# A whole order planned anew, with four single banks open to every product

## The chip, the cores and the metric

The kernel runs on one core of a Trainium2 chip. The metric is the device time of one execution in microseconds (us). Lower is better. Five engines work at once, each through a queue of its own in the order written: TensorE (PE, matrix products), VectorE (DVE), ScalarE (ACT), GpSimd (POOL) and SyncE (SP, which here issues all transfers).

## The reference

An attention of the RWKV-6 kind feeds a two-layer network. For 4 sequences of 768 tokens, with 8 heads of 48:

```python
for t in range(S):
    cur = np.einsum('bhd,bhe->bhde', u[None] * kt, vt)
    y[:, :, t] = np.einsum('bhd,bhde->bhe', rt, state + cur)
    state = wt[:, :, :, None] * state + np.einsum('bhd,bhe->bhde', kt, vt)
# x: y as 3072 tokens x 384
h = x @ w_in          # 384 x 2048
r = np.maximum(h, 0.0)
return (r * r) @ w_out    # 2048 x 384
```

Inputs and output are float32.

## The kernel before

**Steps.** The tokens are cut into 12 steps of 256 (three for each sequence), a step into two chunks (c = 0, 1) of 128. Within a chunk the recurrence becomes matrix products. For each step the kernel loads w, k, r and v (384 KB each), and then: ww_ multiplies neighbouring decays, lw_ takes the logarithm, cum_ sums the logarithms on TensorE, al_ derives the second sum, exp_ takes the exponential, rd_ scales k and r (rd_.s.1 and rd_.s.0) with it. kw_, rw_, ku_, qp_, q_, qs_, vs_, v_ and vq_ are elementwise preparations and casts. The scaled k and r are transposed: on TensorE (tr_, copied out by rkt_) for steps 0 to 3, by transfers (dtr_, two for rT and one for kT) for steps 4 to 11. p_ makes the scores of half the heads, pm_ masks them, su_, ts_ and sn_ carry the state, y_ and yc_ make the output, ysb_ brings it to SBUF, and it is transposed by yt_ and xt_ (steps 0 to 5) or by a transfer, dyt_ (steps 6 to 11).

**Network.** m1_.s.g makes 256 of the 2048 hidden columns of step s: six products of 128x256. rl_ takes the ReLU out of PSUM, sq_.s.q squares a quarter of the hidden columns, m2_.s.c.q multiplies that quarter of chunk c with its part of w_out: four products of 128x384, and four m2_ add up in one bank. os_ copies the sum to SBUF, store writes it. The two weights come in four pieces each (ld.g.i for w_in, ld.g.o for w_out; 768 KB), each cast to bf16 by a cast. Piece g of w_in serves m1_.s.2g and m1_.s.2g+1, piece q of w_out serves m2_.s.c.q.

**Order.** All of it stands in one string, ORDER: a word is an operation, its step and parts, after "=" the engine (A is ACT, V is DVE, G is POOL), after ":" the bank. The kernel issues the words in that order, so each engine's queue is the string's order of its own words. SP's queue holds the loads (ld), stores, dtr_ and dyt_. A word waits in its queue until its inputs are there and its buffer is free; what stands behind it on that engine waits too.

**Banks.** PSUM has two double banks (att, written 0 and 1 by the attention's words) and four single ones: bk (2) and m1_bank (2). m1_ takes only m1_bank, m2_ only bk; p_ and su_ can take "m" or "b", a pair of single banks, in place of a double one. Lines 531 to 571 are m1_, rl_, sq_, m2_ and os_; rl_ is line 545 on ACT and 547 on DVE, sq_ 553 and 555, os_ 568 and 570.

**Dummies.** warm_.n.i issues n products on zeros into a bank; they serve no output. They stand only in the opening, 46 products in 8 words.

**Buffers.** Four for each of the loads w, k, r and v, four for weight pieces on their way to the cast, four for outputs.

Of the kernel before, what the change touches and what calls it, by code (L numbers as in the profile page):

```python
# [17 lines left out]
ld.0.w ld.0.k ld.0.r ld.0.u ld.1.w ww_.0=V lw_.0 warm_.11.5 cum_.0:0 kw_.0=G exp_.0 rd_.0.1 ld.0.v warm_.8.5  # L18
tr_.0.1:0 rkt_.0.1=A ld.1.k ld.1.r rw_.0=G ld.2.w ku_.0=G rd_.0.0 ld.1.v warm_.3.5 tr_.0.0:1 ww_.1=V
rkt_.0.0=A qp_.0=V ld.2.r v_.0=A warm_.5.5 p_.0.0:m p_.0.1:1 ac_.0 lw_.1 q_.0 su_.0:b ld.2.k cum_.1:0  # L20
ts_.0.0=A kw_.1=G pm_.0.0 pm_.0.1 vs_.0.0=A sn_.0.0 ld.1.i exp_.1 rw_.1=G vs_.0.1=A qs_.0=A rd_.1.1 ku_.1=G
warm_.3.2 yc_.0.1:1 ld.0.i ac_.1 ts_.0.1=V rd_.1.0 warm_.2.2 tr_.1.1:0 sn_.0.1 y_.0:1 rkt_.1.1=A vq_.0=V
tr_.1.0:1 ww_.2=G ld.2.i v_.1=A rkt_.1.0=V ysb_.0=V vs_.1.1=A warm_.4.2 p_.1.1:0 qp_.1=G su_.1:m ld.2.v
pm_.1.1 lw_.2 yt_.0:0 cum_.2:1 ld.3.i ts_.1.0=V rw_.2=G q_.1 exp_.2 kw_.2=G xt_.0=V vs_.1.0=A rd_.2.0 qs_.1=G
ac_.2 cast.i.1=A rd_.2.1 warm_.10.1 tr_.2.0:1 sn_.1.0 p_.1.0:0 ku_.2=G ts_.1.1=V yc_.1.1:1 tr_.2.1:0
cast.i.0=A pm_.1.0 ld.0.o m1_.0.3:0 ld.3.w rkt_.2.1=V m1_.0.2:1 vq_.1=G rkt_.2.0=V y_.1:1 rl_.0.3=A yc_.1.0:1
rl_.0.2=V p_.2.0:0 m1_.0.1:0 ld.1.o ysb_.1=V cast.i.2=G m1_.0.0:1 rl_.0.1=A pm_.2.0 yt_.1:0 ld.3.r rl_.0.0=A
m1_.0.5:0 v_.2=A xt_.1=V qp_.2=G sn_.1.1 m1_.0.4:1 rl_.0.5=A p_.2.1:1 su_.2:b sq_.0.0=A rl_.0.4=V ld.2.o
m1_.1.4:0 cast.i.3=G ts_.2.0=V pm_.2.1 m1_.1.5:1 rl_.1.4=A q_.2 sn_.2.0 m1_.1.3:0 rl_.1.5=A ld.3.o vs_.2.1=G
vs_.2.0=A yc_.2.0:0 yc_.2.1:0 rl_.1.3=V m1_.1.6:1 cast.o.0=G qs_.2=A m1_.1.0:0 ld.3.k rl_.1.6=V sq_.0.2=A  # L30
y_.2:0 rl_.1.0=V m1_.1.1:1 vq_.2=G m1_.1.7:0 rl_.1.1=V ld.3.v m2_.0.1.0:0 sq_.1.2=A rl_.1.7=V sq_.0.1=A
cast.o.1=G m1_.1.2:1 rl_.1.2=A ysb_.2=V m1_.0.7:0 ld.4.w ww_.3=G yt_.2:1 rl_.0.7=V m1_.0.6:1 xt_.2=V m2_.0.1.1
sq_.1.1=A rl_.0.6=V ld.5.w m1_.2.6:0 cast.o.2=G lw_.3 sq_.1.0=A rl_.2.6=A cum_.3:1 sq_.1.3=A rw_.3=G al_.3
ld.5.r m2_.0.0.0:1 m1_.2.7:1 m2_.0.0.1 cast.o.3=V exp_.3 sq_.0.3=A ld.4.k rd_.3.0 kw_.3=G m1_.2.1:0 rl_.2.7=A
ac_.3 m2_.0.1.2 m2_.0.0.2 rl_.2.1=V ku_.3=G m2_.0.0.3 rd_.3.1 ld.4.v m2_.0.1.3 vs_.3.0=A m1_.2.0:1 os_.0.1=V
qp_.3=G ld.5.v m1_.2.3:0 os_.0.0=V rl_.2.0=V tr_.3.1:0 rl_.2.3=A tr_.3.0:1 rkt_.3.1=V v_.3=A ld.4.r m1_.2.4:1
ww_.4=G rkt_.3.0=V m2_.1.0.0:0 rl_.2.4=A q_.3 ww_.5=G p_.3.1:0 vs_.3.1=A ld.6.k su_.3:1 pm_.3.1 p_.3.0:m
m2_.1.0.1 ts_.3.0=A lw_.4 sn_.3.0 ld.5.k pm_.3.0 m2_.1.0.2 qs_.3=A m2_.1.1.0:1 sq_.2.0=A vq_.3=G ts_.3.1=V
m2_.1.0.3 ld.6.w cum_.4:0 m2_.1.1.1 ku_.4=G ac_.4 al_.4 store.0.1 m1_.2.5:0 os_.1.0=A v_.5=A yc_.3.1:1 y_.3:1
lw_.5 kw_.4=G m1_.2.2:1 ld.6.r ysb_.3=V rl_.2.5=A m2_.1.1.2 exp_.4 sn_.3.1 rl_.2.2=V yt_.3:0 rw_.4=G cum_.5:1  # L40
xt_.3=V m2_.1.1.3 vs_.4.0=A ac_.5 sq_.2.1=A qp_.4=G al_.5 m1_.3.0:0 rd_.4.1 v_.4=A m1_.3.3:1 rd_.4.0 dtr_.4.1
m2_.2.0.0:0 rl_.3.0=A rw_.5=G rl_.3.3=A m2_.2.0.1 os_.1.1=V exp_.5 q_.4 dtr_.4.0 su_.4:0 sq_.2.2=A m1_.3.4:0
kw_.5=G rd_.5.0 ww_.6=G m2_.2.1.0:1 rl_.3.4=A ts_.4.0=V sq_.2.3=A m1_.3.5:1 vs_.4.1=A rd_.5.1 sn_.4.0
m2_.2.1.1 store.1.0 ts_.4.1=V rl_.3.5=V ku_.5=G m1_.3.6:0 store.1.1 m2_.2.1.2 qs_.4=A ld.7.w ld.6.v rw_.6=G
p_.4.1:1 rl_.3.6=A p_.4.0:0 pm_.4.1 pm_.4.0 m2_.2.1.3 lw_.6 vq_.4=G m1_.3.1:1 m1_.3.2:0 rl_.3.1=A su_.5:1
dtr_.5.1 dtr_.5.0 vs_.5.1=G sq_.3.0=A rl_.3.2=V yc_.4.0:0 yc_.4.1:0 sn_.4.1 y_.4:0 os_.2.1=V sq_.3.1=A
m1_.3.7:1 ysb_.4=V ld.7.v m2_.2.0.2 rl_.3.7=A ld.8.w kw_.6=G vs_.5.0=G yt_.4:1 ld.7.k sq_.3.3=A m2_.2.0.3
xt_.4=V cum_.6:0 al_.6 m1_.4.4:0 qp_.5=G os_.2.0=A ac_.6 m1_.4.7:1 ts_.5.0=V exp_.6 rl_.4.4=V m2_.3.0.0:1
rl_.4.7=A rd_.6.1 m1_.4.6:0 rd_.6.0 m2_.3.0.1 dtr_.6.1 m2_.3.1.0:0 ku_.6=G qp_.6=G sq_.3.2=A rl_.4.6=A q_.5
dtr_.6.0 p_.5.0:1 p_.5.1:0 vs_.6.0=A m1_.4.5:1 sn_.5.0 m2_.3.0.2 qs_.5=G rl_.4.5=A pm_.5.1 pm_.5.0 vq_.5=G  # L50
m1_.4.1:0 m1_.4.3:1 rl_.4.3=A store.2.1 ld.8.v m2_.3.0.3 rl_.4.1=V ld.8.k v_.6=A ww_.7=G y_.5:0 q_.6 os_.3.0=A
ld.7.r m1_.4.0:1 store.0.0 ld.9.k ww_.8=G yc_.5.0:0 qs_.6=A su_.6:1 yc_.5.1:0 ysb_.5=V vs_.6.1=A ts_.6.0=V
m1_.4.2:0 ld.8.r m2_.3.1.1 rl_.4.0=V yt_.5:1 xt_.5=V sn_.6.0 lw_.7 vq_.6=G rl_.4.2=A p_.6.0:0 m2_.3.1.2
sq_.4.3=A store.2.0 pm_.6.0 m1_.5.2:1 ku_.7=G m1_.5.6:0 ts_.6.1=V yc_.6.1:0 sq_.4.0=A rl_.5.2=A p_.6.1:1
rl_.5.6=A m2_.3.1.3 kw_.7=G pm_.6.1 sq_.4.2=A m1_.5.4:1 rw_.7=G m1_.5.3:0 os_.3.1=V rl_.5.4=A y_.6:0 sn_.6.1
rl_.5.3=A cum_.7:1 kw_.8=G ysb_.6=V al_.7 m2_.4.0.0:1 vs_.7.1=A m1_.5.7:1 m1_.5.5:0 v_.7=G dyt_.6 sq_.4.1=A
rl_.5.7=V qp_.7=G rl_.5.5=V m2_.4.1.0:0 exp_.7 ld.9.w ld.9.v m2_.4.0.1 ac_.7 rd_.7.0 sq_.5.1=A m2_.4.0.2
ku_.8=G rd_.7.1 sq_.5.3=A dtr_.7.0 m2_.4.0.3 m1_.5.0:1 lw_.8 m1_.5.1:0 rw_.8=G rl_.5.0=V su_.7:0 q_.7
rl_.5.1=A cum_.8:1 dtr_.7.1 m1_.6.3:1 qs_.7=A m1_.6.5:0 rl_.6.3=V ld.10.w qp_.8=G ac_.8 sq_.5.0=A m2_.4.1.1
os_.4.0=V ts_.7.0=V ld.11.w sn_.7.0 m1_.6.4:1 rl_.6.5=A al_.8 ww_.9=G m2_.4.1.2 ld.9.r rl_.6.4=V exp_.8  # L60
store.3.0 m2_.5.1.0:1 sq_.5.2=A rd_.8.1 ts_.7.1=V sn_.7.1 m1_.6.0:0 vs_.7.0=G vs_.9.1=A rd_.8.0 m2_.4.1.3
m2_.5.1.1 kw_.9=G rl_.6.0=A dtr_.8.0 p_.7.1:0 v_.8=A p_.7.0:1 vq_.7=G pm_.7.1 m1_.6.1:1 m2_.5.1.2 rl_.6.1=A
pm_.7.0 ku_.9=G m2_.5.1.3 sq_.6.0=A lw_.9 m1_.6.6:0 dtr_.8.1 store.3.1 q_.8 yc_.7.0:0 v_.9=A yc_.7.1:0
rl_.6.6=V rw_.9=G su_.8:1 y_.7:0 os_.5.1=A ts_.8.0=V m1_.6.2:1 ysb_.7=V os_.4.1=A cum_.9:1 m1_.6.7:0 al_.9
dyt_.7 m2_.5.0.0:1 rl_.6.2=V exp_.9 ww_.10=G rl_.6.7=V m2_.5.0.1 ac_.9 ld.10.r rd_.9.1 sq_.6.1=A sq_.6.2=A
sn_.8.0 qp_.9=G ld.10.k qs_.8=G store.4.1 m2_.5.0.2 ld.10.v rd_.9.0 m2_.5.0.3 m2_.6.1.0:0 vs_.8.1=G sq_.6.3=A
dtr_.9.0 vs_.8.0=A p_.8.0:m p_.8.1:0 pm_.8.0 su_.9:1 m2_.6.1.1 ts_.9.0=A pm_.8.1 m2_.6.1.2 lw_.10 m1_.7.4:0
rw_.10=G os_.5.0=V m1_.7.0:1 rl_.7.4=V sn_.9.0 vq_.8=G yc_.8.1:0 dtr_.9.1 yc_.8.0:0 rl_.7.0=V y_.8:0 m1_.7.1:0
q_.9 rl_.7.1=A ts_.9.1=V m2_.6.1.3 kw_.10=G ysb_.8=V m1_.7.7:1 sq_.7.0=A ww_.11=G cum_.10:1 dyt_.8 rl_.7.7=V
m1_.7.5:0 qs_.9=A al_.10 m2_.6.0.0:1 v_.10=G rl_.7.5=A m1_.7.2:1 exp_.10 ld.11.k vs_.9.0=G m2_.6.0.1 lw_.11  # L70
rd_.10.0 rd_.10.1 m1_.7.3:0 rl_.7.2=A vq_.9=G ac_.10 m2_.6.0.2 os_.6.1=A rl_.7.3=A vs_.10.0=A store.6.1
m1_.7.6:1 store.5.1 ku_.10=G m2_.6.0.3 vs_.10.1=A ld.11.r sn_.9.1 rl_.7.6=V m1_.8.5:0 dtr_.10.0 p_.9.1:0
rl_.8.5=A p_.9.0:1 qp_.10=G pm_.9.1 m1_.8.3:1 m2_.7.0.0:0 rl_.8.3=A pm_.9.0 m1_.8.4:0 sq_.7.1=A m1_.8.2:1
os_.6.0=A y_.9:0 sq_.7.3=A rl_.8.2=V yc_.9.1:0 rw_.11=G su_.10:1 m2_.7.1.0:1 sq_.7.2=A ts_.10.0=V ysb_.9=V
m2_.7.1.1 rl_.8.4=A ku_.11=G q_.10 m1_.8.7:1 dyt_.9 m1_.8.1:0 rl_.8.7=V cum_.11:0 dtr_.10.1 kw_.11=G sn_.10.0
rl_.8.1=A m2_.7.1.2 al_.11 m1_.8.0:1 exp_.11 ld.11.v qs_.10=G ts_.10.1=V sn_.10.1 vq_.10=G m1_.8.6:0 rl_.8.0=A
store.6.0 rd_.11.0 m2_.7.1.3 rl_.8.6=A rd_.11.1 m1_.9.4:1 sq_.8.0=A ac_.11 dtr_.11.0 m1_.9.1:0 qp_.11=G
rl_.9.4=V sq_.8.2=A m2_.7.0.1 os_.7.1=V p_.10.1:1 sq_.8.1=A p_.10.0:0 pm_.10.1 store.5.0 dtr_.11.1 store.7.1
m1_.9.0:1 v_.11=G pm_.10.0 vs_.11.1=G m2_.8.1.0:1 rl_.9.0=A rl_.9.1=A m2_.8.1.1 sq_.8.3=V m1_.9.5:1 m2_.7.0.2
m2_.7.0.3 os_.7.0=A yc_.10.0:1 yc_.10.1:1 rl_.9.5=V su_.11:0 y_.10:1 m1_.9.2:0 ysb_.10=V m1_.9.6:1 rl_.9.2=A  # L80
ts_.11.0=V dyt_.10 m2_.8.0.0:0 rl_.9.6=V sn_.11.0 m1_.9.3:0 q_.11 m2_.8.1.2 rl_.9.3=A yc_.11.0:1 vs_.11.0=A
p_.11.1:0 yc_.11.1:1 p_.11.0:m m2_.8.0.1 pm_.11.0 m2_.8.0.2 pm_.11.1 sq_.9.1=A m2_.8.0.3 m2_.8.1.3 qs_.11=A
# [549 lines left out]
```

## Time and profile before

| | us |
|---|---|
| median of three runs | 183.11 |
| lowest and highest run | 182.49, 183.14 |
| span of the profiled execution | 182.2 |
| PE busy | 171.8 |
| ACT busy | 132.7 |
| DVE busy | 130.0 |
| POOL busy | 122.7 |

The page of the profile gives the span (first to last instruction) and no time of its own for that execution; the median stands 0.91 us above the span. The granted TensorE clock has a mean of 0.997. The 16 DMA engines are busy at a share of 85.9% for the transfers that the kernel issues. In rows of the timeline the first number is the start, the second the length; "[1.84 <-DMA ...]" is idle time before the row and what ended it. In rows of the windows stand the stretch, its length, the busy time of PE, PEld (weight loads), DVE, ACT and POOL with counts, the granted clock, the DMA share and GB/s. In rows of groups stand line, engine, operation, tiles, shapes and count, then busy time and mean ns, then idle time before the group.

### The profile page before, as it was taken

How to read it: one execution, taken by the hardware profiler on the slowest of the kernel's cores; microseconds unless marked ns; L12 is line 12 of the kernel's file. 1: busy time of each engine (PE TensorE's matmuls, PEld its weight loads, DVE VectorE, ACT ScalarE, POOL GpSimd, SP SyncE). 2: the span in 40 equal slices, each digit the busy share in tenths (PEclk: the TensorE clock that was granted, in tenths of full speed). 3: DMA queues.
4: the chain of work that ended last, by engine and by line, in shares of the span. 5: the costliest groups of instructions: out<-in, count | busy, mean ns of one | idle time of the engine just before them, and what ended most of it. 6: DMA issues, size and time to landing. Idle time of an engine off the chain costs nothing.

```text
span 182.2 us, 5695 instructions
## 1 busy us (share of the span) xinstructions
PE 171.8 (94%) x2385; PEld 123.4 (68%) x2385; DVE 130.0 (71%) x195; ACT 132.7 (73%) x235; POOL 122.7 (67%) x140
## 2 busy tenths in 40 slices
...
GB/s 138 263 263 240 221 359 350 337 314 311 234 274 230 261 158 270 99 247 130 239 296 205 193 270 172 252 189 193 171 109 195 150 47 0 86 144 33 0 86 130
DMA packets 79208, 35.81 MB, mean 197 GB/s; under 512 B 72400, under 2 KB 77648, under 8 KB 79184
## 3 DMA queue, kind: packets, MB, share of 16 engines
q1 hardware_dynamic: 79184, 35.46, 85.9%
q8 instruction: 18, 0.29, 0.7%
...
## 4 chain that ended last, share of the span: by engine, by line
PE 75%; SPq 10%; DMA 8%; ACT 4%; issue 1%; DVE 1%; ACTq 0%
PE bk L561 32%; PE m L536 32%; SPq L178 8%; DMA w_st<-in_moe_w_in_dram 5%; PE att L420 3%; DMA rT<-rdec_buf 2%; PE att L483 2%; PE att L493 2%; PE att L446 1%; ACT gt L545 1%; PE att L326 1%; ACT wi_sb L200 1%; PE bk L516 1%; SPq L188 1%; SPq L205 1%
## 5 line engine op out<-in xcount | busy, mean ns | idle before, releaser
L536 PE MATMUL m<-xT,wi_sb 128*128 128x256 bf16 x576 | 74.0, 273 | 1.3 <-ACT gt L545 1.2
L561 PE MATMUL bk<-wo_sb,gt 128*128 128x384 bf16 x384 | 71.9, 326 | 0.0
L536 PEld LDWEIGHTS <-wi_sb 128*128 128x128 bf16 x576 | 54.8, 98 | 13.0 <-issue 0.9
L561 PEld LDWEIGHTS <-gt 128*128 128x128 bf16 x384 | 36.9, 98 | 19.2
L545 ACT ACTIVATE gt<-m 128x512 f16<-128x512 f32 x56 | 33.0, 595 | 22.3 <-PE m L536 21.9
L553 ACT ACTIVATE gt<-gt 128x1024 bf16<-128x1024 f16 x42 | 43.3, 1051 | 1.4 <-DVE gt L547 1.1
L547 DVE TENSOR_SCALAR gt<-m 128x512 f16<-128x512 f32 x40 | 27.0, 686 | 9.6 <-PE m L536 9.3
L434 DVE TENSOR_TENSOR pmT<-att,mask 128x1024 bf16<-128x1024 f32 x20 | 23.9, 1218 | 4.5 <-PE att L420 4.5
L297 POOL TENSOR_TENSOR ku<-k_raw,u_bc 128x768 f32<-128x768 f32 x12 | 21.8, 1819 | 0.2 <-DMA u_bc<-in_u_dram 0.2
L302 POOL TENSOR_TENSOR ku<-ku,r_raw 128x768 f32<-128x768 f32 x11 | 20.7, 1881 | 0.2
L316 POOL TENSOR_TENSOR ku<-v_sh,qs 128x768 f32<-128x768 bf16 x11 | 16.3, 1479 | 4.9 <-ACT qs L277 4.8
L277 ACT CAST v_sh<-v_raw 64x384 bf16<-64x384 f32 x34 | 17.3, 508 | 0.4
L290 POOL TENSOR_TENSOR k_raw<-k_raw,w_raw 128x384 f32<-128x384 f32 x12 | 12.2, 1013 | 6.4 <-DMA k_raw<-in_k_dram 6.3
L286 POOL TENSOR_TENSOR r_raw<-r_raw,w_raw 128x384 f32<-128x384 f32 x12 | 12.0, 1000 | 6.4 <-DMA r_raw<-in_r_dram 6.4
L504 DVE TENSOR_TENSOR y_sb<-att,ku 128x768 bf16<-128x768 f32 x12 | 11.4, 953 | 5.5 <-issue 1.6
L461 POOL TENSOR_TENSOR S<-t_state,ac_buf 128x192 bf16<-128x192 f32 x20 | 10.2, 512 | 6.4 <-DVE t_state L456 3.4
L361 DVE TENSOR_TENSOR kdec_buf<-k_raw,att 128x768 bf16<-128x768 f32 x12 | 11.4, 949 | 3.4 <-ACT att L340 2.8
L358 DVE TENSOR_TENSOR rdec_buf<-r_raw,att 128x384 bf16<-128x384 f32 x24 | 12.1, 547 | 2.2 <-ACT att L340 1.1
L340 ACT ACTIVATE att<-att 128x768 f32<-128x768 f32 x12 | 9.6, 798 | 3.1 <-PE att L328 1.9
L568 ACT ACTIVATE o_sb<-bk 128x384 f32<-128x384 f32 x13 | 6.3, 485 | 7.4 <-PE bk L561 7.3
L307 DVE TENSOR_REDUCE q<-ku 128x16 f32<-128x768 f32 x12 | 11.3, 943 | 0.0
L578 PE MATMUL att<-warm 128*128 128x512 bf16 x27 | 9.1, 492 | 1.2 <-DVE half_ones L228 1.2
...
## 6 DMA issues: line engine op xcount, KB each, us to landing
w_raw<-in_w_dram SPq DMA_DIRECT2D x12, 384.0 KB, 5.3
k_raw<-in_k_dram SPq DMA_DIRECT2D x12, 384.0 KB, 5.9
r_raw<-in_r_dram SPq DMA_DIRECT2D x12, 384.0 KB, 5.7
v_raw<-in_v_dram SPq DMA_DIRECT2D x12, 384.0 KB, 5.8
...
w_st<-in_moe_w_in_dram SPq DMA_DIRECT2D x4, 768.0 KB, 11.1
...
rT<-rdec_buf SPq DMA_TRANSPOSE x16, 4.1
```

The source lines that it names most:

```text
L178: nc.sync.dma_start(out=t[:, hs, at:at + 2, :].rearrange("p h j d -> p h (j d)"), in_=src[b, hs, i * T:(i + 1) * T, :].rearrange("h (p j) ...
L277: copy(out[j * Q:(j + 1) * Q, c], src[c * Q:(c + 1) * Q, :, j])
L290: tensor_mul("kw_", s, h)(raw["k", s][:, hs, 0, :], raw["k", s][:, hs, 1, :], raw["w", s][:, hs, 1, :])
L297: tensor_mul("ku_", s, h)(tiles["ku", s][:, hs], raw["k", s][:, hs, 1:3, :], u_bc[:, hs, None, :].to_broadcast([C, n, 2, D]))
L302: tensor_mul("qp_", s, h)(ku, ku, raw["r", s][:, heads(h), 0:2, :])
L316: tensor_mul("vq_", s)(vq[:], tiles["vs", s][:], tiles["qs", s][:, :, :, None].to_broadcast([C, 2, H, D]))
L434: nc.vector.tensor_mul(pmT, ps_p[:].rearrange("p e (x t) -> p (e x) t", t=C), mk.to_broadcast([C, 8, C]))
L536: nc.tensor.matmul(ps1[:, j, :], wi_sb[:, n // 4, kk, n % 4 * 128:(n % 4 + 1) * 128], tiles["xT", s][:, :, kk, :], start=(kk == 0), stop=( ...
L545: nc.scalar.activation(rl, m1, AF.Relu, scale=RS)
L547: nc.vector.tensor_scalar(out=rl, in0=m1, scalar1=RS, scalar2=0.0, op0=ALU.mult, op1=ALU.max)
L553: nc.scalar.activation(gt, rl, AF.Square)
L561: nc.tensor.matmul(m2, gt[:, n, c * C:(c + 1) * C], wo_sb[:, n, :], start=(n == 0), stop=(n == NT - 1))
```

## The change

It replaces the string ORDER, opens all four single banks to m1_ and m2_ alike (the list `quad`), and lets the four quarters of an m2_ sum come in any order: the first quarter issued starts the sum and the fourth ends it, counted in `summed`.

```diff
+    quad = bk + m1_bank
...
     def m1_(s, g):
-        ps1 = tiles["m1", s, g] = m1_bank[int(slot["m1_", s, g])][:].rearrange("p (j t) -> p j t", j=2)
+        ps1 = tiles["m1", s, g] = quad[int(slot["m1_", s, g])][:].rearrange("p (j t) -> p j t", j=2)
...
+    summed = {}
+
     def m2_(s, c, q):
         gt = tiles["gt", s]
-        m2 = bk[int(slot["m2_", s, c])][:, 0:DM]
-        for n in range(4 * q, 4 * q + 4):
-            nc.tensor.matmul(m2, gt[:, n, c * C:(c + 1) * C], wo_sb[:, n, :],
-                             start=(n == 0), stop=(n == NT - 1))
+        m2 = quad[int(slot["m2_", s, c])][:, 0:DM]
+        summed[s, c] = summed.get((s, c), 0) + 1
+        for n in range(4):
+            nc.tensor.matmul(m2, gt[:, 4 * q + n, c * C:(c + 1) * C], wo_sb[:, 4 * q + n, :],
+                             start=(summed[s, c] == 1 and n == 0), stop=(summed[s, c] == NT // 4 and n == 3))
```

The products, copies and transfers are the same in number; what differs is their order, and on which engine some run:

| words | before: ACT, DVE, POOL | after |
|---|---|---|
| rl_ (96) | 56, 40, 0 | 73, 23, 0 |
| sq_ (48) | 42, 6, 0 | 31, 17, 0 |
| os_ (24) | 13, 11, 0 | 16, 8, 0 |
| kw_, rw_, ku_, qp_ (48) | 0, 1, 47 | 0, 15, 33 |
| vs_ (24) | 17, 0, 7 | 13, 2, 9 |
| v_ (12) | 9, 0, 3 | 5, 0, 7 |
| dummy products | 46 in 8 words | 55 in 12 words |

The order of loads in the opening, before and after:

```
before 0.w 0.k 0.r 0.u 1.w 0.v 1.k 1.r 2.w 1.v 2.r 2.k 1.i 0.i 2.i 2.v 3.i 0.o 3.w 1.o 3.r 2.o 3.o 3.k 3.v
after  0.w 0.k 0.r 0.u 1.k 1.w 1.r 0.v 1.v 2.r 2.w 2.k 1.i 0.i 2.v 2.i 3.w 3.i 3.k 3.r 1.o 3.v 2.o 4.w 3.o 0.o
```

TensorE's words from the first m1_ on, before and after:

```
before m1_.0.3 m1_.0.2 y_.1 yc_.1.0 p_.2.0 m1_.0.1 m1_.0.0 yt_.1 m1_.0.5 m1_.0.4 p_.2.1 su_.2 ...
after  m1_.0.2 tr_.2.1 m1_.0.3 yt_.1 p_.2.1 p_.2.0 m1_.0.1 m1_.1.0 m1_.1.3 m1_.0.0 yc_.2.0 m1_.1.2 y_.2 su_.2 m1_.1.1
       m1_.1.5 m1_.1.4 yc_.2.1 m1_.0.5 m1_.0.4 cum_.3 m1_.0.7 m1_.0.6 ...
```

and SP's words around steps 6 to 8 after:

```
dtr_.6.0 dtr_.6.1 ld.7.w ld.7.k store.1.0 ld.7.v ld.7.r ld.8.w ld.8.k ld.8.r dyt_.6 dtr_.7.0 store.0.1 dtr_.7.1
ld.8.v dtr_.8.0 store.2.1 dtr_.8.1 ld.9.w
```

m1_.0.6 takes bank 3 of the quad, which rl_.0.4 on ACT empties; m1_.0.1 takes bank 2. The dummies ahead of cum_.0 are 13 instead of 11.

More of the change, by code (lines that the diff above doesn't have):

```diff
@@ L17 @@
 ORDER = """
[L18 to L82, printed above, removed]
```

91 lines of the change are left out of this document (78 added, 13 removed).

## The prediction

> **What bounds the kernel now.** I read the page's head and its chain first, then the chain in order of time, then the windows.
>
> ```profile
> span 182.2 us, 5695 instructions
> PE 171.8 (94%) x2385; PEld 123.4 (68%) x2385; DVE 130.0 (71%) x195; ACT 132.7 (73%) x235; POOL 122.7 (67%) x140
> PE 75%; SPq 10%; DMA 8%; ACT 4%; issue 1%; DVE 1%; ACTq 0%
> ```
>
> ```profile
> 18.96 9.57 DMA w_st<-in_moe_w_in_dram
> 28.55 1.47 ACT wi_sb L200
> 30.02 0.51 ACT gt L545
> 30.57 1.47 PE m L536 x12
> 32.04 0.33 PE bk L516 x6
> 32.38 1.31 PE m L536 x12
> 33.69 0.36 PE att L420 x16
> 40.04 0.65 PE bk L561 x4
> 171.68 7.16 PE bk L561 x44
> 178.91 0.49 ACT o_sb L568
> ```
>
> ```profile
> 20.00:30.00 10.00, 7.97 (x178) 5.53 (x177) 9.64 (x15) 6.31 (x10) 7.88 (x10) 1.00 0.99 314
> 80.00:90.00 10.00, 9.45 (x190) 7.29 (x187) 7.24 (x10) 7.73 (x16) 8.77 (x13) 1.00 1.03 193
> 140.00:150.00 10.00, 10.00 (x188) 7.24 (x187) 7.07 (x10) 5.14 (x9) 3.58 (x5) 1.00 0.46 105
> ```
>
> The chain has two parts. Up to 28.55 it is transfers: the second piece of the first weight lands, is cast for 1.47 us, a ReLU frees a bank, and at 30.57 the products resume. From there to the output copy at 178.91 TensorE carries it, at full granted clock, and the only idle time that the windows show is 0.55 us in 80 to 90. The tail, 182.2 - 178.91 = 3.3 us, is one copy and one store, and the change ends with the same pair. So the products behind the opening can't get shorter; the change can win where they begin and in that 0.55, and it can lose anywhere. Prices on TensorE: six products of the first matrix 1.31 / 2 = 0.655, four of the second 0.65, transposes of y 0.33, half of the attention scores (p) 0.36 alone.
>
> **The opening.** Both kernels move the same twelve loads ahead of the first weight pieces (pieces 1 and 0), so I leave 28.55 where it is. Before, the next m1_ needed a bank that rl_.0.3 on ACT had to empty, and that waited behind the cast:
>
> ```profile
> 28.55 1.47 ACT L200 CAST wi_sb<-w_st 128x1536 bf16<-128x1536 f32 x1 [1.84 <-DMA w_st<-in_moe_w_in_dram]
> ```
>
> After, m1_.0.1 has a third bank, and rl_.0.3 is on DVE. It starts when the cast ends, 30.02, plus the 0.04 between 30.02 + 0.51 and 30.57: 30.06, so **0.51 sooner**. By then yt_.1 and one p_ more have run (before, they ran at 32.04 and 33.69): **0.33 + 0.36**. Gain 1.20. The cover: DVE must have finished rkt_.2.1, rl_.0.3 and xt_.1. It is busy 9.64 of 10 there; counting its queue from the landing of the third load, I get xt_.1 at about 29.8, needed at 30.72, so 0.9 us spare. The lower end of this gain is 0 (DVE late by 2 us), the upper 1.20.
>
> The dummies: 13 instead of 11 ahead of cum_.0, 55 instead of 46 in all.
>
> ```profile
> 1.19 4.87 PE L578 MATMUL att<-warm 128*128 128x512 bf16 x11 [1.19 <-DVE half_ones L228]
> 5.85 0.29 PE L324 MATMUL att<-half_ones,lw_buf 128*128 128x2 bf16 x4
> ```
>
> Eleven took 4.87, 0.44 each, and ended as cum_.0 began; two more move cum_.0, and all of step 0 behind it, by 0.88. This is inside the 29.8 above. The other seven stand where TensorE waits; I take 0 for them, since 28.55 hides step 0 to 2. If that cover is gone they cost 7 x 0.44 = 3.1 at most. Less than nothing they can't give: the clock is 1.00 already.
>
> **The weights' second half and ACT.** After, pieces 2 and 3 of the first weight stand one load later each, and m2_ takes quarter 1 first, then 2, 3, 0, as they land; the products need piece 2 only after eight m1_ instead of four. I count no wait there. ACT takes 73 rl_ instead of 56, and 31 sq_ instead of 42.
>
> ```profile
> L545 ACT ACTIVATE gt<-m 128x512 f16<-128x512 f32 x56 | 33.0, 595 | 22.3 <-PE m L536 21.9
> L553 ACT ACTIVATE gt<-gt 128x1024 bf16<-128x1024 f16 x42 | 43.3, 1051 | 1.4 <-DVE gt L547 1.1
> L277 ACT CAST v_sh<-v_raw 64x384 bf16<-64x384 f32 x34 | 17.3, 508 | 0.4
> L268 ACT ACTIVATE lw_buf<-ww 128x384 bf16<-128x384 f32 x12 | 6.2, 519 | 2.3 <-DVE ww L264 2.2
> ```
>
> From the end of m1_.0.1 at 30.72 its queue is seven rl_ (0.1, 1.0, 1.2, 0.0, 1.1, 1.5, 1.4), two sq_, one vs_ (two casts) and lw_.3, then rl_.0.4: 8 x 0.595 + 2 x 1.051 + 1.02 + 0.52 = 8.4, so bank 3 is free at 39.1. TensorE in the same time has eleven m1_ (7.2) and about 1.4 of attention, and wants bank 3 for m1_.0.6 at 38.7. **Wait 0.4** (0 to 1.2, if two more rl_ come late). Behind it TensorE holds everything, since its products go in order.
>
> **The middle.** Attention moves forward by 2 to 11 us against the products from step 4 on, with the transposes of steps 4 to 11 on SP's queue between loads and stores. Before, step 6 waited for them, and step 7 came out just even:
>
> ```profile
> 86.65 0.21 PE L420 MATMUL att<-rT,kT 64*64 64x128 bf16 x1 [0.19 <-DMA rT<-rdec_buf]
> 87.23 0.42 PE L420 MATMUL att<-rT,kT 64*64 64x128 bf16 x15 [0.36 <-DMA rT<-rdec_buf]
> 92.50 0.24 PE L324 MATMUL att<-half_ones,lw_buf 128*128 128x2 bf16 x4
> ```
>
> ```profile
> 97.58 2.99 SPq L401 DMA_TRANSPOSE rT<-rdec_buf  x2
> 100.67 1.26 SPq L403 DMA_TRANSPOSE kT<-kdec_buf  x1
> ```
>
> ```profile
> 105.40 0.58 PE att L420 x32
> ```
>
> ```profile
> kT<-kdec_buf SPq DMA_TRANSPOSE x8, 4.6
> ```
>
> cum_.7 at 92.50, the last transpose at 100.67, landed 4.6 later at 105.3, used at 105.40. After, step 6 has 14 us between cum_ and p_ (11.4 before), so the **0.55 goes**. Step 7 is the narrow one. Its room: eleven m1_ and five m2_ (10.45), y_, su_, two cum_ and yc_ (1.66): 12.12. Its chain, from these rows:
>
> ```profile
> L358 DVE TENSOR_TENSOR rdec_buf<-r_raw,att 128x384 bf16<-128x384 f32 x24 | 12.1, 547 | 2.2 <-ACT att L340 1.1
> L361 DVE TENSOR_TENSOR kdec_buf<-k_raw,att 128x768 bf16<-128x768 f32 x12 | 11.4, 949 | 3.4 <-ACT att L340 2.8
> L504 DVE TENSOR_TENSOR y_sb<-att,ku 128x768 bf16<-128x768 f32 x12 | 11.4, 953 | 5.5 <-issue 1.6
> L570 DVE TENSOR_SCALAR o_sb<-bk 128x384 f32<-128x384 f32 x11 | 6.0, 550 | 4.9 <-PE bk L561 4.9
> L333 DVE SCALAR_TENSOR_TENSOR att<-att,lw_buf 128x384 f32<-128x384 f32 x9 | 5.1, 563 | 2.5 <-PE att L326 1.4 <-ACT ac_buf L346 1.0
> ```
>
> ```profile
> L574 SPq DMA_DIRECT2D out_dram<-o_sb x24: 332/477/2628, 59.2 to 179.4; - x24
> ```
>
> cum_ 0.3, then on DVE al_, os_, ysb_, rd_.1 and the two of rd_.0: 0.56 + 0.55 + 0.95 + 0.95 + 1.09 = 4.4 in all; dyt_.6 runs on SP meanwhile; then the rT pair 2.99, a store 0.48, and 4.6 for kT: 12.48. **Wait 0.36**; with the store's longest issue, 2.63, it is 2.5, and with none of these late it is 0. By the Trainium skill, "DMA: Bandwidth & Descriptors", section on the anatomy of one DMA, a transfer costs about 2.0 us fixed plus its bytes at 436 GB/s, which for these 256 KB would be an estimated 2.6 and no wait, a saving of 0.36 more; the page fits that to transfers issued by GpSimd, and the 4.6 of this trace decides.
>
> ```profile
> 68.18 0.41 SPq L178 DMA_DIRECT2D w_raw<-in_w_dram  x1
> ```
>
> Loads: before, ld.7.w is issued 24 us ahead of cum_.7; after, it stands behind all of step 6's transposes. Counted from cum_.6: DVE's queue to rd_.6.0 5.0, the rT pair 2.99, kT 1.3, then the load, its product on POOL and its logarithm:
>
> ```profile
> w_raw<-in_w_dram SPq DMA_DIRECT2D x12, 384.0 KB, 5.3
> ```
>
> ```profile
> L264 POOL TENSOR_TENSOR ww<-w_raw 128x384 f32<-128x384 f32 x10 | 9.9, 1001 | 0.0
> ```
>
> 5.3 + 1.0 + 0.52 makes 16.1, and TensorE reaches cum_.7 after 22 pieces of products and 4.9 of attention, 19.2. Spare 3.1. The same count for ww_.8, which stands behind ku_.7, kw_.7, rw_.7 and v_.7 on POOL, leaves 2.2. No wait by medians.
>
> **The sum.** 1.20 + 0.55 - 0.4 - 0.36 = 0.99 off the span of 182.2: 181.2. The page gives no time of that execution beside the span; the median, 183.11, is 0.91 above it, and I take that to lie around it. Forecast 182.1.
>
> **Rivals.** *The gain is eaten* (p 0.26): DVE, the busiest engine of the opening, is late and the start stays near 30.57 (loses up to 1.2), or the transposes of steps 7 and 8 each cost half a microsecond more. For it: 9.64 of 10, and the even step 7 before. Against: 0.9 spare. Time 182.6 to 184.0, near 183.1.
>
> *Loads come late* (p 0.35, the other side): the shorter leads on SP's queue. Place: ld.7.w to ww_.8, then the same for step 8. One long issue is in the trace:
>
> ```profile
> 69.59 3.29 SPq L403 DMA_TRANSPOSE kT<-kdec_buf  x1
> ```
>
> against 1.26 above: 2.0 late; with one store at 2.63 instead of 0.48 another 2.15. From 2.2 us of lateness on it decides. 4.15 - 2.2 = 2.0 of wait at cum_.8, as much again a step later, since cum_ holds every product behind it: 182.1 + 3.9 = 186.0, or 184.1 with only one step hit. For it: DMA shares near 1.0 until 130. Against: TensorE reached 178.91 without such a wait before, in the same traffic.
>
> *The change doesn't do what it says*: more banks give nothing. Before, TensorE lost only 0.55 after 30.57, so only the 0.51 of the bank at the start is at stake; this lies within the first rival.
>
> **The numbers.** A measurement can tell 0.5%, 0.92 us, from no change: below 182.19 is faster, above 184.03 slower. The forecast's case has 0.39 and spreads from 181.3 (both waits gone, 1.75 gained) to 182.2. The eaten gain has 0.26, all of it same; late loads 0.35, slower. Range 181.2 to 185.7: it takes in the best sum, and leaves out the worst of the late loads. Both signs hold much; the likeliest case alone is 181.3 to 182.2.
>
> **What would show it.** In the changed profile: the second m1_ stretch starts at 30.0 to 30.1 straight behind the cast; a wait for ACT's ReLU near 38.7, under half a microsecond; p_.6 without a wait on rT; at p_.7 a wait on kT of about 0.4; TensorE full elsewhere. I am wrong if the windows between 40 and 140 show TensorE idle by more than 1 us in all, above all at the cum_ products, or if the start has not moved.

## The result, and the profile after

The changed kernel takes **188.68 us** (median of four runs, 187.54 to 189.0), beside 182.8 for the kernel before in the same session: ratio 1.0321, 95% interval 1.0281 to 1.0362. It is slower by 5.9 us. The forecast was 182.1, with a range up to 185.7.

The head of the page after (an execution of 187.54 us), and its chain:

```profile
span 185.6 us, 5708 instructions
PE 175.0 (94%) x2389; PEld 124.0 (67%) x2394; DVE 140.3 (76%) x206; ACT 126.9 (68%) x226; POOL 114.6 (62%) x140
PE 64%; POOL 16%; SPq 6%; DVE 4%; DMA 4%; issue 3%; ACT 1%; POOLq 0%
```

The span is 3.4 us longer, less than the 5.9 between the medians: this is the fastest of the four executions, and the profiled one of the kernel before was a late one (the account below says how that is seen). And 16% of the chain lies on POOL, which did not appear in the chain before although POOL now has 8 us less to do. DVE has 10 us more. Three rows of the chain in order of time, and the idle time of TensorE behind 28 us by what ended it:

```profile
35.99 0.84 issue
37.55 1.48 POOL ku L318
61.13 1.78 POOL ku L299
```

```profile
PE att L326 <- DVE y_sb L506: 1.7, 1, 1.7
PE att L485 <- DVE pmT L436: 1.0, 1, 1.0
PE att L448 <- POOL v_bf L274: 0.6, 1, 0.6
PE bk L518 <- DVE y_sb L506: 0.5, 1, 0.5
```

No line names a load, a transpose or a ReLU, the waits that the forecast priced. The releasers are elementwise words on DVE and POOL. Now one row of the windows for each kernel, from the start of the second stretch of m1_ to the end of the last product: before, then after (the second number is the length, the third TensorE's busy time, with its count).

```profile
30.57:178.91 148.34, 147.60 (x2031) 109.93 (x2030) 106.12 (x157) 112.78 (x199) 101.61 (x107) 1.00 0.85 187
```

```profile
28.36:182.36 154.00, 149.98 (x2015) 109.34 (x2009) 117.32 (x168) 106.34 (x187) 92.99 (x109) 1.00 0.83 183
```

The stretch starts 30.57 - 28.36 = 2.21 sooner. It has 154.00 - 149.98 = 4.02 of idle time instead of 0.74: 3.28 more. And TensorE is busy 149.98 instead of 147.60, 2.38 longer, though yt_.1 and one p_ (0.33 + 0.36) already lie ahead of it. The end moves by -2.21 + 3.28 + 2.38 = +3.45, from 178.91 to 182.36. So there are three things to explain: the start, the waits, and products that take longer at full clock. The newly opened banks are not the third: six products of m1_ take 0.66 to the next start in bk (40.42 to 41.08), as in m.

### The profile page after: what moved, and what is told of

Its sections match the earlier page's. It is cut to its first block, busy times and chain, and to the rows that moved or that the text cites. A ratio compares the mean times of both kernels' runs of the same rounds, so it can differ in the third digit from the quotient of the medians.

```text
span 185.6 us, 5708 instructions
## 1 busy us (share of the span) xinstructions
PE 175.0 (94%) x2389; PEld 124.0 (67%) x2394; DVE 140.3 (76%) x206; ACT 126.9 (68%) x226; POOL 114.6 (62%) x140
## 4 chain that ended last, share of the span: by engine, by line
PE 64%; POOL 16%; SPq 6%; DVE 4%; DMA 4%; issue 3%; ACT 1%; POOLq 0%
PE m L566 16%; PE bk L538 14%; PE bk L566 13%; PE m L538 11%; SPq L180 6%; DMA w_raw<-in_w_dram 4%; POOL ww L266 3%; PE att L485 2%; PE att L422 2%; POOL v_sh L279 2%; POOL r_raw L288 2%; PE att L495 2%; POOL ku L299 2%; POOL wo_sb L202 2%; DVE pmT L436 1%
## 5 line engine op out<-in xcount | busy, mean ns | idle before, releaser
L538 PE MATMUL bk<-xT,wi_sb 128*128 128x256 bf16 x306 | 40.7, 273 | 0.1
L566 PE MATMUL m<-wo_sb,gt 128*128 128x384 bf16 x208 | 38.8, 326 | 0.0
L538 PE MATMUL m<-xT,wi_sb 128*128 128x256 bf16 x270 | 35.9, 273 | 0.0
L566 PE MATMUL bk<-wo_sb,gt 128*128 128x384 bf16 x176 | 34.1, 327 | 0.0
L555 ACT ACTIVATE gt<-gt 128x1024 bf16<-128x1024 f16 x31 | 32.2, 1052 | 1.6 <-DVE gt L549 1.3
L547 ACT ACTIVATE gt<-m 128x512 f16<-128x512 f32 x36 | 21.1, 597 | 13.8 <-PE m L538 13.6
L547 ACT ACTIVATE gt<-bk 128x512 f16<-128x512 f32 x37 | 21.9, 596 | 11.6 <-PE bk L538 11.2
L557 DVE TENSOR_TENSOR gt<-gt 128x1024 bf16<-128x1024 f16 x17 | 13.3, 816 | 0.7 <-ACT gt L547 0.6
L266 POOL TENSOR_TENSOR ww<-w_raw 128x384 f32<-128x384 f32 x9 | 10.7, 1187 | 4.5 <-DMA w_raw<-in_w_dram 4.5
L549 DVE TENSOR_SCALAR gt<-bk 128x512 f16<-128x512 f32 x14 | 9.5, 687 | 4.1 <-PE bk L538 2.0
```

Of the source, the lines that this page charges most:

```text
L266: tensor_mul("ww_", s, h)(tiles["ww", s][:, hs], raw["w", s][:, hs, 0, :], raw["w", s][:, hs, 1, :])
L538: nc.tensor.matmul(ps1[:, j, :], wi_sb[:, n // 4, kk, n % 4 * 128:(n % 4 + 1) * 128], tiles["xT", s][:, :, kk, :], start=(kk == 0), stop=( ...
L547: nc.scalar.activation(rl, m1, AF.Relu, scale=RS)
L555: nc.scalar.activation(gt, rl, AF.Square)
L557: nc.vector.tensor_mul(gt, rl, rl)
L566: nc.tensor.matmul(m2, gt[:, 4 * q + n, c * C:(c + 1) * C], wo_sb[:, 4 * q + n, :], start=(summed[s, c] == 1 and n == 0), stop=(summed[s, ...
```

## The experiments

Ratios are to the kernel before, run beside each; the changed kernel has 1.0321.

**Order and engine letters swapped.** 113 words have another engine in the two orders. In one run the old order gets the new letters, in the other the new order the old ones, for example

```diff
-kw_.4=G   ku_.4=G   qp_.4=G   sq_.2.0=A
+kw_.4=V   ku_.4=V   qp_.4=V   sq_.2.0=V
```

> The order of before, each word on the engine that the change gives it (113 words differ). Theory 1 (engines): the elementwise words moved from GpSimd to VectorE slow both engines down while they run side by side, so 2 us or more slower than before (185 or more), with longer rows on both in 30 to 70 us. Theory 2 (order): the loss lies in how TensorE's words follow each other, which is here that of before: within 1 us of before.

> The changed order, each word on the engine that it had before. Theory 1: 3 us or more faster than the changed kernel (185.5 or less), TensorE idle under 1.5 us between 30 and 70. Theory 2: TensorE's busy time from the start of the stream stays 2 to 3 us above that of before, and the time stays above 187.

Measured: 196.2 us (1.0764, 1.0724 to 1.0804) and 225.62 us (1.2355, 1.2304 to 1.2405). Both far off, the second most of all. An order is made for its letters: with other letters each engine's queue holds its words in an order nobody planned, and in the second run TensorE waited 6.9 us at one cum_ alone. The swap says nothing about which half of the change costs, and I give it no weight.

**POOL relieved of three words and DVE of one in the changed kernel.** On POOL these are eight casts and copies, on DVE two casts; all go to ACT.

```diff
-vs_.2.1=V  vs_.3.1=G  vs_.3.0=G  qs_.3=G
+vs_.2.1=A  vs_.3.1=A  vs_.3.0=A  qs_.3=A
```

> The changed kernel with four words of steps 2 and 3 moved to ScalarE: vs_.2.1 from VectorE, vs_.3.0, vs_.3.1 and qs_.3 from GpSimd. Theory 1: GpSimd's queue, which is followed without a gap from 35 to 67 us, gets 4.7 us shorter ahead of ww_.5, TensorE's idle time in 30 to 70 falls from 4.0 us to 2 or less, and the time falls by about 2 us. Theory 2: less than 0.5 us.

187.9 us (1.0308, 1.0257 to 1.0359): no gain that can be told. The wait at y_.2 is gone, but its place is taken:

```profile
PE m L538 <- ACT gt L547: 2.4, 1, 2.4
PE att L326 <- DVE y_sb L506: 1.7, 1, 1.7
PE att L422 <- DMA kT<-kdec_buf: 0.8, 1, 0.8
```

ACT's queue now holds the four casts of vs_.3 and the four copies of qs_.3, from 46.35 to 49.26, with the ReLU behind them that empties the bank. The wait of 1.7 stays. The load on POOL was not the whole cause. The timeline of the changed kernel shows more. First POOL, then DVE (start, length):

```profile
50.05 2.85 POOL L279 CAST v_sh<-v_raw 64x384 bf16<-64x384 f32 x4
52.95 1.83 POOL L279 COPY qs<-q 64x8 f32<-64x8 f32 x4
56.30 1.72 POOL L266 TENSOR_TENSOR ww<-w_raw 128x384 f32<-128x384 f32 x1
```

```profile
51.59 2.45 DVE L557 TENSOR_TENSOR gt<-gt 128x1024 bf16<-128x1024 f16 x3
54.90 2.26 DVE L299 TENSOR_TENSOR ku<-k_raw,u_bc 128x768 f32<-128x768 f32 x1
57.19 1.64 DVE L304 TENSOR_TENSOR ku<-ku,r_raw 128x768 f32<-128x768 f32 x1
58.75 0.94 DVE L506 TENSOR_TENSOR y_sb<-att,ku 128x768 bf16<-128x768 f32 x1
```

ww takes 1.72 on POOL (1.00 before), ku 2.26 on DVE for the same 768 columns that y_sb does in 0.94. y_sb reads one operand from PSUM; ku, qp and the squares read both from SBUF. Before, DVE had no word with two SBUF operands between 30 and 67 us.

**Squares against ReLU on DVE.** Six words of 43 to 67 us in the kernel before go from ACT to DVE: in one run squares (both operands in SBUF), in the control ReLU of like length (operand in PSUM).

```diff
-sq_.1.3=A sq_.0.3=A sq_.2.0=A sq_.2.1=A sq_.2.2=A sq_.2.3=A
+sq_.1.3=V sq_.0.3=V sq_.2.0=V sq_.2.1=V sq_.2.2=V sq_.2.3=V
```

```diff
-rl_.2.6=A rl_.2.7=A rl_.2.3=A rl_.2.4=A rl_.2.5=A rl_.3.0=A
+rl_.2.6=V rl_.2.7=V rl_.2.3=V rl_.2.4=V rl_.2.5=V rl_.3.0=V
```

> The kernel before with six squares of 43 to 67 us on DVE in place of ACT; a square on DVE has both its inputs in SBUF. Theory 1 (such a word and a POOL word hold each other up): POOL's rows between 43 and 67, 1.00 for 384 columns and 1.81 for 768, rise to 1.3 to 1.7 and 2.2 to 2.6 where a square runs, the squares take over 0.73 in the mean, and POOL, which is full from 60 to 70, is late for TensorE: 0.5 to 2.5 us slower than the kernel before. Rival (DVE has only more to do): POOL's rows stay, squares at 0.73, time within 0.5 of the kernel before.

> The control for the squares: six ReLU of the same stretch on DVE in place of ACT, 0.69 each, with their input in PSUM. Theory 1: POOL's rows stay at 1.00 and 1.81; time within 0.5 of the kernel before, or up to 1 slower by DVE's own queue. Rival (any load on DVE does it): the same stretching as with the squares.

184.69 us (1.0083, 1.0047 to 1.0119) with the squares, 183.43 (1.0021, 0.9994 to 1.0048) with the ReLU. The groups of 40 to 72 us with the squares, and then with the ReLU:

```profile
L297 POOL TENSOR_TENSOR ku<-k_raw,u_bc 128x768 f32<-128x768 f32 x3 | 6.3, 2116 | 0.0
L555 DVE TENSOR_TENSOR gt<-gt 128x1024 bf16<-128x1024 f16 x6 | 7.8, 1293 | 0.0
L361 DVE TENSOR_TENSOR kdec_buf<-k_raw,att 128x768 bf16<-128x768 f32 x3 | 2.8, 939 | 0.0
```

```profile
L297 POOL TENSOR_TENSOR ku<-k_raw,u_bc 128x768 f32<-128x768 f32 x3 | 5.5, 1819 | 0.0
L547 DVE TENSOR_SCALAR gt<-m 128x512 f16<-128x512 f32 x13 | 8.6, 683 | 0.9 <-PE m L536 0.9
```

A square on DVE takes 1.29 in the mean instead of 0.73, and POOL's ku 2.12 instead of 1.82; beside the ReLU POOL keeps 1.82, and words with a PSUM operand (kdec, 0.94) keep theirs in both. Single rows of the run with the squares show how it goes:

```profile
55.10 1.47 POOL L316 TENSOR_TENSOR ku<-v_sh,qs 128x768 f32<-128x768 bf16 x1 [0.75 <-ACT qs L277]
56.54 2.28 POOL L297 TENSOR_TENSOR ku<-k_raw,u_bc 128x768 f32<-128x768 f32 x1
```

```profile
55.18 1.95 DVE L555 TENSOR_TENSOR gt<-gt 128x1024 bf16<-128x1024 f16 x1
65.27 0.68 DVE L555 TENSOR_TENSOR gt<-gt 128x1024 bf16<-128x1024 f16 x1
```

POOL's word starts first and runs its usual 1.47, to 56.57 (55.10 + 1.47). The square, issued at 55.18, ends 0.56 after that, at 57.13 (55.18 + 1.95), as if it had stood still until POOL was done. POOL's next word takes 2.28 instead of 1.82, about as much longer as the square still runs beside it. In these rows the second one stands. The Trainium skill says this in "SBUF — State Buffer", section "Who interferes with whom": a DVE instruction with two SBUF inputs contends with a GpSimd instruction that reads SBUF, the first one holds the shared ports for its whole length, and a DVE instruction with at most one SBUF input, outside the modes that use both ports, does not contend. These rows agree on each of the three points: 1.29 and 2.12 with the squares, the square's end 0.56 behind POOL's, and 1.82 unchanged beside the ReLU.

**The same cure in the changed kernel, in three steps.** ysb_.3 ahead of qp_.4 on DVE; then, separately, five squares of 48 to 54 us back to ACT with five ReLU given to DVE for them; then both, with vs_.2.1 on ACT.

```diff
-qp_.4=V sq_.2.2=A ysb_.3=V
+sq_.2.2=A ysb_.3=V qp_.4=V
```

```diff
-sq_.0.3=V sq_.0.2=V sq_.2.0=V sq_.1.3=V sq_.2.1=V  rl_.2.7=A rl_.2.1=A rl_.2.3=A rl_.2.5=A rl_.2.4=A
+sq_.0.3=A sq_.0.2=A sq_.2.0=A sq_.1.3=A sq_.2.1=A  rl_.2.7=V rl_.2.1=V rl_.2.3=V rl_.2.5=V rl_.2.4=V
```

> The changed kernel with one word moved on DVE: the sum of step 3's output (ysb_.3) runs ahead of qp_.4 instead of behind it. Theory 1 (waits in 30 to 67 come from DVE's and POOL's queues): ysb_.3 ends 1.6 us sooner, the 1.69 us wait of cum_.5 goes, TensorE idle of 28 to 70 falls from 4.0 to about 2.4, and the kernel is 1.0 to 1.6 us faster than the changed one. Rival (the wait passes to the next word, su_.4 behind v_.4): under 0.5.

> The changed kernel with the five squares of 48 to 54 us on ACT in place of DVE and five ReLU of the same stretch on DVE in place of ACT: as many operations on each, but DVE no longer reads two operands from SBUF beside POOL there. Theory 1: POOL's four v_sh casts fall from 2.85 to about 2.1 and its four qs copies from 1.83 to 0.9, POOL is 1.5 to 2 us sooner at vq_.3, and the kernel is 0.8 to 1.8 us faster than the changed one. Rival (DVE is simply too full): rows as before, under 0.5.

> Both of these and vs_.2.1 on ACT in the changed kernel. Theory 1: nearly all of the 3.3 us of added waits goes, 2.0 to 3.2 us faster than the changed kernel. Theory 2 (ten more pieces of attention at 0.19 us each, by the run with spread pieces): about 2 us stay on TensorE whatever the queues do, which the earlier start roughly pays for, so it ends between 183 and 185 us, not below the kernel before. Rival (pieces cost nothing): 181 to 182.5.

The first gives 188.94 us (1.0361, 1.0327 to 1.0394), no gain: the wait of cum_.5 falls to 0.69, and the next word takes it over.

```profile
58.71 0.25 PE L326 MATMUL att<-half_ones,lw_buf 128*128 128x2 bf16 x4 [0.69 <-ACT lw_buf L270]
63.90 0.44 PE L448 MATMUL att<-v_bf,kdec_buf 64*64 64x48 bf16 x32 [1.60 <-POOL v_bf L274]
```

v_.4 ends on POOL when POOL's queue lets it: at 63.7 in the changed kernel, at 63.8 here. Here the rival was right; the idle time in all is 4.74, not less than 4.02. The second run gives 188.27 (1.0337, 1.0278 to 1.0397), no gain either, although its rows do what was expected:

```profile
49.83 2.14 POOL L279 CAST v_sh<-v_raw 64x384 bf16<-64x384 f32 x4
52.03 1.15 POOL L279 COPY qs<-q 64x8 f32<-64x8 f32 x4
```

2.85 becomes 2.14, 1.83 becomes 1.15, and vq_.3 starts 1.6 sooner. But a ReLU is now late on DVE (0.87 us of wait) and kT is 1.0 late behind 70 us, and the idle time in all is 4.49. All three together give 185.83 (1.0205, 1.0173 to 1.0237), 2 us less than the changed kernel by the ratios. Its window:

```profile
28.48:180.79 152.31, 149.62 (x2016) 109.53 (x2009) 112.24 (x166) 109.44 (x190) 90.88 (x109) 1.00 0.83 185
```

This is a little above the 183 to 185 that the second theory gave; the 2.0 to 3.2 us of the first theory was met as well. Idle 2.69 instead of 4.02; busy 149.62, still 2.02 more than before the change. Of the 1.33 of idle time that went, 1.0 is the wait at y_.2: it is gone here and in the run that relieved POOL, the two with vs_.2.1 on ACT, and stands unchanged in the two others. So letters and one place in a queue take back part of the waits, and not mainly by way of the squares; the longer busy time hardly moves with them.

**What a piece of attention costs TensorE.** p_, su_ and yc_ are products on 64x64 of the array; m1_, m2_, y_ and the rest use 128x128. Behind the third m1_ the old order has 21 unbroken pieces of such half-array words, the new one 32: eleven more, where two of the expectations say 14 and ten. Two probes in the tail of the kernel before add 192 half-array products on zeros, in one piece or sixteen behind each of twelve product words.

```diff
+    def half_(i):          # 16 products: warm 64x64, 48 columns
-m1_.10.2 m1_.10.7 m2_.9.1.1 ...
+half_.0 half_.1 ... half_.11 m1_.10.2 m1_.10.7 ...      (one piece)
+m1_.10.2 half_.0 m1_.10.7 half_.1 m2_.9.1.1 half_.2 ... (spread)
```

> The kernel before with 192 half-array products (64x64, 48 columns, on zeros, results not used) added in one piece in the tail. Both theories: 192 x about 0.017 of new columns per product, so 2 to 4 us more than the kernel before; it is the base for the run with the same products spread.

> The same 192 half-array products, sixteen behind each of twelve product words of the tail instead of in one piece: eleven more pieces. Theory 2 (pieces of attention between the products cost TensorE time): 1.2 to 1.6 us slower than the run in one piece, 0.11 to 0.14 for each piece more, which over the 14 more pieces of the changed kernel is 1.5 to 2.0 of its 2.4 us of longer busy time. Rival (a piece costs nothing): within 0.3 of it.

Both take 186.77 us (1.0221, 1.0153 to 1.0289, and 1.0241, 1.0192 to 1.0291), which looks like the rival. The rows tell otherwise. In one piece, then spread:

```profile
158.10 1.40 PE L588 MATMUL att<-warm 64*64 64x48 bf16 x148
161.23 0.66 PE L588 MATMUL att<-warm 64*64 64x48 bf16 x44 [1.74 <-issue]
161.83 2.74 PE L537 MATMUL m<-xT,wi_sb 128*128 128x256 bf16 x12
```

```profile
166.84 0.83 PE L537 MATMUL m<-xT,wi_sb 128*128 128x256 bf16 x6
167.60 0.31 PE L588 MATMUL att<-warm 64*64 64x48 bf16 x16
167.85 0.83 PE L537 MATMUL m<-xT,wi_sb 128*128 128x256 bf16 x6
```

Spread, a product word and sixteen half products take 167.85 - 166.84 = 1.01, where the word alone takes 0.65: 0.35 a group. In one piece the twelve groups take 161.83 - 158.00 = 3.83 (the word ahead starts at 157.35 and takes 0.65), of which 1.74 is a pause that the profile puts to nothing but issue; 2.09 / 12 = 0.17 a group is left. The difference, 0.18 to 0.19, is the price of a piece by these rows. Whether the pause hid it in the medians is not known: only one execution in one piece was profiled, and the four lie apart, two at 186.0 and two at 187.5 and 188.1. The times of this pair decide nothing. The half products start 0.76 after the word ahead of them instead of 0.65, so the price lies on both sides. It does not come with few columns alone: y_ has 48 as well, on the whole array, and the twelve products ahead of a y_ take the usual 1.31 to its start (26.99 to 28.30 before). Real words answer the question without the pause: nine pieces of the kernel before are split by one product word next to them.

```diff
-p_.4.1:1 ... p_.4.0:0 ... m2_.2.1.3
+p_.4.1:1 ... m2_.2.1.3 p_.4.0:0 ...      (and eight more)
```

> The kernel before with nine pieces of attention from step 4 on split in two, by one product word that stood next to them: the same words on TensorE, nine pieces more, nothing else moved. Theory 2 (a piece of half-array products costs TensorE 0.19 us): 1.4 to 2.0 us slower than the kernel before, without a wait to show for it, in longer busy time behind 60 us. Rival (the longer busy time of the changed kernel has another cause): within 0.4 of the kernel before.

184.43 us (1.0118, 1.0088 to 1.0149), 1.6 to 2.7 us slower.

```profile
29.72:179.83 150.11, 149.53 (x2031) 109.25 (x2030) 106.29 (x158) 112.64 (x200) 101.70 (x107) 1.00 0.81 185
```

Idle 0.58, not more than the 0.74 before; busy 149.53 instead of 147.60 with the same words: 1.93 / 9 = 0.21 a piece. One split piece shows it by itself:

```profile
105.05 0.43 PE L420 MATMUL att<-rT,kT 64*64 64x128 bf16 x16
105.41 0.83 PE L536 MATMUL m<-xT,wi_sb 128*128 128x256 bf16 x6
106.17 0.43 PE L420 MATMUL att<-rT,kT 64*64 64x128 bf16 x16
106.53 1.48 PE L561 MATMUL bk<-wo_sb,gt 128*128 128x384 bf16 x8
```

The two halves of the scores and the product word take 106.53 - 105.05 = 1.48 here, and unsplit 106.58 - 105.33 = 1.25 in the kernel before (its rows stand further below): 0.23 more. Eleven pieces more are 2.4 us, the 2.38 of the changed kernel; with the 0.69 of work that it has already done, some 0.7 stays over. Most of that may be waits after all, by an estimate: a row ends about 0.16 behind the place where the next could start (0.82 against 0.66 above), so every wait counts 0.16 too short as idle time and as much too long as busy time, and the changed kernel has about four such places more. The Trainium skill, "TensorEngine Tiling (Array Packing)", section "Tiling Modes", has the rule: changing the tiling mode drains TensorE. It gives no price; if that drain is what these rows show, it is 0.2 us here for the way there and back.

**The opening by itself.** First the order of the first 14 loads alone, put into the kernel before:

```diff
-ld.0.w ld.0.k ld.0.r ld.0.u ld.1.w ld.0.v ld.1.k ld.1.r ld.2.w ld.1.v ld.2.r ld.2.k ld.1.i ld.0.i
+ld.0.w ld.0.k ld.0.r ld.0.u ld.1.k ld.1.w ld.1.r ld.0.v ld.1.v ld.2.r ld.2.w ld.2.k ld.1.i ld.0.i
```

> The kernel before with the first 14 loads in the changed order, nothing else. Theory (the earlier start of the stream in the changed kernel comes from the order of its loads): piece 0 of the first weight is cast at about 26.4 instead of 28.55, and the time falls by 1.5 to 2 us. Rival (that landing differs from execution to execution, or goes with other things): cast within 0.5 us of 28.55, time as before.

186.18 us (1.0213, 1.0187 to 1.0238). The weights are issued 1.9 us sooner, as in the changed kernel, but ld.0.v lands later and TensorE stands still for it:

```profile
15.27 0.47 PE L446 MATMUL bk<-v_bf,kdec_buf 64*64 64x48 bf16 x32 [3.64 <-ACT v_bf L272]
```

```profile
10.00:20.00 10.00, 6.32 (x120) 3.29 (x118) 6.87 (x9) 6.33 (x16) 5.31 (x7) 0.83 1.24 269
20.00:30.00 10.00, 7.41 (x92) 3.92 (x90) 9.64 (x13) 6.18 (x10) 7.84 (x10) 0.83 0.95 325
```

The granted clock has a mean of 0.83 in each of these slices (in windows of 15.6 to 18.9 and 25.8 to 29.1 it is 0.50, between them 1.00), and the second stretch starts later than before, at 33.43. The changed kernel fills that place with dummies. Next its whole opening, up to m1_.0.1 and pm_.2.0, with the rest of the old order behind it:

```diff
-(the old opening) ... m1_.0.0:1 rl_.0.1=A ...
+(the new opening) ... rl_.0.2=A m1_.0.1:2 pm_.2.0 | ld.3.i ld.0.o ld.3.w ld.1.o cast.i.2=G m1_.0.0 rl_.0.1=A ... (old order)
```

> The changed kernel's opening, up to its third product of the first matrix and pm_.2.0 (load order, dummies, the four banks, yt_.1 and both p_ of step 2 ahead), and from there the order, the banks and the engines of the kernel before. Theory (the opening alone gains, and what the changed kernel loses comes from its order and engines behind 30 us): second stretch of products at 28.3 to 28.6, no new wait behind it, 0.6 to 1.9 us faster than the kernel before, 1.2 the likeliest. Rival (an earlier start only runs into the casts and loads of the later weight pieces): within 0.5 of the kernel before.

182.95 us (1.0023, 0.9996 to 1.0051): no gain. Here too the rival was right:

```profile
31.70 1.48 PE L538 MATMUL m<-xT,wi_sb 128*128 128x256 bf16 x12 [1.58 <-POOL wi_sb L202]
```

The second stretch starts at 28.63, and after two words it needs the third weight piece, which lands at 30.18 and is cast until 31.64. The last run puts four products of step 1, which need only the first two pieces, in between:

```diff
-m1_.0.0 m1_.0.5 m1_.0.4 su_.2 m1_.1.4 m1_.1.5 ...
+m1_.0.0 m1_.1.3 m1_.1.0 su_.2 m1_.1.1 m1_.1.2 m1_.0.5 m1_.0.4 ...
```

> The run with the changed opening before the old order, and behind m1_.0.0 the four products of step 1 that need only the first two weight pieces (m1_.1.3, .1.0, .1.1, .1.2) ahead of those that need the third, which POOL casts until 31.6; squares follow their ReLU. Theory (the start's gain was lost to the 1.58 us wait for that cast): the wait falls to 0 to 0.3, 0.8 to 1.6 us faster than the run without it, 181.3 to 182.1 beside a kernel before of 182.4. Rival (an earlier start only meets the next late load or cast): a wait of 1 us or more appears before 80 us, and the time stays within 0.5 of the run without it.

**181.43 us**, ratio 0.9934 (0.9904 to 0.9964): faster than both kernels. The wait is gone, and the old order behind it keeps TensorE full (0.52 of idle time):

```profile
28.37:176.07 147.70, 147.18 (x2016) 109.21 (x2009) 105.87 (x157) 112.61 (x200) 100.36 (x106) 1.00 0.83 190
```

So the opening of the change is a gain, 1.3 us by the medians, if the order behind it suits; what the changed kernel loses lies behind it.

## Why the prediction was wrong

**The step that failed** is "the products behind the opening can't get shorter": true, but the sum then took their length as fixed, 147.6 us of busy time and no wait outside the few that it priced. They got 2.38 longer and waited 3.28 more.

- *Pieces, costed at nothing.* The prediction moved attention "forward by 2 to 11 us against the products" and counted its transfers, not how often it now breaks into the products: 32 times instead of 21. At 0.21 to 0.23 a piece that is some 2.4 us, shown by the split pieces. Part of the price stood in the timeline of before: six products take 0.67 to the start of the next words where those are whole-array ones, and 0.75 where they are half-array ones.

```profile
105.33 0.65 PE L420 MATMUL att<-rT,kT 64*64 64x128 bf16 x32
105.91 0.83 PE L536 MATMUL m<-xT,wi_sb 128*128 128x256 bf16 x6
106.58 1.46 PE L561 MATMUL bk<-wo_sb,gt 128*128 128x384 bf16 x8
107.88 0.82 PE L536 MATMUL m<-xT,wi_sb 128*128 128x256 bf16 x6
108.63 0.44 PE L493 MATMUL att<-S,rT 64*64 64x48 bf16 x32
```

- *Elementwise words moved to DVE, costed at nothing.* ku, kw, qp of step 4 and five squares went to DVE, where they read two operands from SBUF while POOL is full. The forecast followed DVE's queue in the opening and at step 7, with the durations of the kernel before, and no queue but ACT's between 30 and 70 us. That the waits there end on elementwise words of DVE and POOL is shown by the list of waits, and that such words and POOL's hold each other up by squares against ReLU. That the one made the other is not shown: five squares taken off DVE shortened POOL's rows and left 4.49 us of idle time. Three repairs together took 1.33 us of it and 2 us of the time away, 1.0 of it by one pair of casts that stood ahead of pm_ in DVE's queue. How much is contention and how much the queues' order stays open; every single repair passed its wait on to another word.
- *The start, undersized.* Forecast 30.06, measured 28.36. "Both kernels move the same twelve loads ahead" was true of the loads but not of their times: the first piece is issued at 15.73, before at 17.59. Nor does the stretch start behind the cast of the second piece, as forecast: that cast ends at 27.87 (26.40 + 1.47), and TensorE runs without a gap from 25.58, just behind the cast of the first, to 28.36 and on.

```profile
17.59 2.40 SPq L188 DMA_DIRECT2D w_st<-in_moe_w_in_dram  x3
```

```profile
15.73 3.37 SPq L190 DMA_DIRECT2D w_st<-in_moe_w_in_dram  x2
```

- *The profiled execution taken for the usual one.* Five other profiles with the old opening start the second stretch at 28.97 to 29.73, not 30.57, and the kernel's runs lie 1.7 to 1.9 us above their span (182.52 with 180.7, 181.44 with 179.7), not 0.91. The page's execution was a late one, so part of the gain at the start was only its lateness, and its own time was, by this estimate, near 184.0, not 183.1. These two errors are smaller than the others, and the second partly undoes the first: against 28.97 to 29.73 the start is 0.6 to 1.4 sooner, not 2.2.
- *Right:* step 6 waits for no transpose any more (the 0.55 goes), and the dummies cost the start nothing: the last end at 25.5, when the cast of the first piece ends too.
- *Priced and absent:* ACT's ReLU at m1_.0.6 (0.4) and kT at p_.7 (0.36). Neither stands among the waits. But kT at p_.7 does in all four runs that alter the changed kernel's letters or DVE's queue, with 0.70 to 0.97: the forecast had this wait right in kind, and undersized.

**The rivals.** "Loads come late" had the sign and named cum_ as a place where all products stand behind a wait; a cum_ did wait longest (1.7). But ld.7.w, 11 us later than before, kept nobody waiting: no row of TensorE behind 70 us names a load. It was right by its sign and wrong by its mechanism. The test that I had set, over 1 us of idle between 40 and 140, was met: the waits of 40.08, 59.75 and 63.73 alone are 2.8.
